# The first batch's attention probabilities turned and normalised on TensorE instead of by DMA, in a fused float32 kernel of attention and two expert layers

## The chip, the cores and the metric

The kernel runs on one core of a Trainium2 chip. The metric is the device time of one execution in microseconds (us). Engines are called by their names: TensorE (PE in the profile, its weight loads PEld), VectorE (DVE), ScalarE (ACT), GpSimd (POOL) and SyncE (SP), whose queue issues the DMAs.

## The reference

Causal attention with an additive bias from running sums, over 4 batches, 8 heads, 576 positions and 64 values a head, and then two expert layers on the 2304 tokens of 512 values, all in float32.

```python
scores = scale * np.matmul(q, k.transpose(0, 1, 3, 2))
cum = np.cumsum(np.maximum(s, 0.0), axis=-1)
bias = -(cum[:, :, :, None] - cum[:, :, None, :])
scores = np.where(causal, -1e9, scores + np.minimum(bias, 0.0))
scores = scores - np.max(scores, axis=-1, keepdims=True)
attn = np.exp(scores)
attn = attn / (np.sum(attn, axis=-1, keepdims=True) + 1e-09)
x = np.matmul(attn, v)            # then (B*S, H*D) = (2304, 512)
h = x @ w_in                      # 512 -> 2048
g = s * np.maximum(h, 0.0) ** 2 + b
x = g @ w_out                     # 2048 -> 512
return ((x @ w_a) * (x @ w_b)) @ w_out2   # 512 -> 1536 -> 512
```

## The kernel before

Nearly every product is made with operands split into a high and a low part, so that three fast matmuls stand for one float32 product. The work runs in four stages, and each stage's tail lies beside the next one's head.

*First halves.* `first_half(i)` (L596) handles the first 256 queries of group `i`; a batch has two groups of four heads, and a group two pairs of heads. So `i < 2` is the first batch, with four pairs, called pairs 0 to 3 here. For a pair, the scores of two query tiles are made (`ti = 1`: queries 128 to 255 against 256 keys; `ti = 0`: queries 0 to 127 against 128 keys), two heads each, by a float32 matmul (L626) and one that adds the mask (L627), into one PSUM bank of the tag `t_s` for each tile. VectorE takes the row maximum (L631, L635). ScalarE makes the exponentials into a float32 tile `p` (L642, tag `t_p0` with five buffers, four a pair) and their sums; VectorE makes the reciprocals `rc` (L556, L557), with a factor of 32768 in them. `split_p` (L526) multiplies the probabilities by `rc` and splits them into a high float16 part on ScalarE (L540) and a low one on VectorE (L542), both in the tile `hl` (tags `t_hl0[0]` and `t_hl0[1]`, three buffers each). SyncE then issues a DMA transpose for each query tile (L652), which puts the blocks of 128 keys by 128 queries into `tr`. The value product `av` (L576, in `value_product`, L561) multiplies `tr` by the values, split into three bfloat16 parts, and ScalarE and VectorE split its result into the expert's input `x` (L587, L589).

*Weights of the first expert.* They come as 16 slices of 1 MB; ScalarE and VectorE decode each from 64-bit numbers (L450 to L462) and split it (L470, L471). The even slices lie in the tag `t_w` before decoding, the odd ones in `t_raw`, which has one buffer.

*First expert.* For each chunk of 256 tokens and each pair of slices `h_unit` (L850, matmuls L861) makes the hidden values into a bank of `t_h`, `elementwise` (L828) squares and splits them, and `y_unit` (L868, matmuls L881) adds their product to two banks of `t_y`. Chunk 0 is the first batch's 256 queries: it needs the input `x` of all four pairs. The chunks that follow are the other batches' first queries, then the second halves (`second_half`, L708), and then the second expert follows.

The order of instructions on each engine is fixed before the kernel runs. Each piece of work is an `op` of the class `Plan` with an engine, a cost, a priority, the buffers that it reads and writes and, as `room`, further buffers that it claims. `Plan.order` plays the work through with these costs and writes the instructions out in the order in which they start there; a lower priority number goes first, and the matmuls of the first expert have 1000 added (`M`), so they yield to any attention work that is ready. A tag hands its buffers to tiles in the order of their creation, unless it says otherwise. On the chip each engine works through its own list in that order and waits by semaphores.

Of the kernel before, what the change touches and what calls it, by code (L numbers as in the profile page):

```python
# [8 lines left out]
F32 = mybir.dt.float32  # L9
# [5 lines left out]
ALU = mybir.AluOpType  # L15
# [4 lines left out]
P = 128  # L20
N = 256
# [6 lines left out]
PE, DVE, ACT, POOL, SP = "PE", "DVE", "ACT", "POOL", "SP"  # L28
# [194 lines left out]
def lin(a, b):  # L223
    return lambda n: a + b * n
# [3 lines left out]
ACT_SB, ACT_PS, ACT_EX = lin(0.30, 0.00064), lin(0.14, 0.00086), lin(0.35, 0.00086)  # L228
DVE_SB2, DVE_PS, DVE_1 = lin(0.17, 0.00102), lin(0.09, 0.00106), lin(0.10, 0.00056)
# [4 lines left out]
def fused_kernel(  # L234
# [15 lines left out]
    nc = tc.nc  # L250
# [13 lines left out]
    op = plan.op  # L264

    def as32(ap):
        return ap.bitcast(F32)
# [38 lines left out]
    t_y = tag(ps_mm, [P, 512], F32, 2, "y")  # L306
# [24 lines left out]
    ident = atc.tile([P, P], F32R, name="ident")  # L331
# [4 lines left out]
    masks, sb = Buf(None, "masks", 1), Buf(None, "sb", 1)  # L336
# [12 lines left out]
    t_hl0 = {i: tag("att0", [P, 4 * (i + 1), P], F16, 3, f"hl{i}") for i in range(2)}  # L349
# [58 lines left out]
    def light_pos(i):  # L408

        return 0.0 + 5.0 * i if i < 2 else 14.0 + 9.0 * (i - 2) if i < 4 else 50.0 + 14.0 * (i - 4)  # L410
# [185 lines left out]
    def first_half(i):  # L596

        b, g = divmod(i, 2)
        kq, rv, vt = light[i]

        def op_tiles():
            a = kq.view()
            return [a[:, j].rearrange("p (x h n) -> p x h n", x=2, h=2) for j in range(2)]

        for x in range(2):
            p = 2 * g + x
            pr = light_pos(i) + 2.5 * x
            x_t[b, p] = Buf(t_x, f"xs{b}{p}")
            tr = Buf(t_tr0, f"tr0{b}{p}")
            nm = f"0{b}{p}"  # L610

            nmx, sm, rc = (Buf(t_sm0[n], f"{n}{nm}") for n in ("nm", "sm", "rc"))
            tiles = {}
            for ti in (1, 0):
                w = (ti + 1) * P
                bank = Buf(t_s, f"s{nm}{ti}")
                at = 2 * (1 - ti)

                def view(bank=bank, w=w):
                    return bank.t.rearrange("p (h n) -> p h n", h=2)[:, :, :w]  # L620

                def go(ti=ti, w=w, x=x, view=view):
                    kt, qt = op_tiles()
                    for h in range(2):
                        o = view()[:, h]
                        nc.tensor.matmul(o, qt[:66, x, h, ti * P : (ti + 1) * P], kt[:66, x, h, :w], start=True, stop=False)  # L626
                        nc.tensor.matmul(o[:, w - P : w], ident, mask1, start=False, stop=True)  # L627

                hl = Buf(t_hl0[ti], f"hl{nm}{ti}")
                op(PE, 2 * (w / 600 + 0.08), pr, go, r=[kq, masks], w=[bank], late=0.15, room=[hl])  # L630
                op(DVE, DVE_PS(2 * w), pr, lambda at=at, nmx=nmx, view=view: nc.vector.tensor_reduce(  # L631
                    out=nmx.t[:, at : at + 2], in_=view(), axis=AX.X, op=ALU.max, negate=True
                ), r=[bank], w=[(nmx, ti)])
                tiles[ti] = w, bank, at, view, hl
            op(DVE, 0.17, pr, lambda nmx=nmx: nc.vector.tensor_scalar_mul(nmx.t, nmx.t, SCALE), w=[nmx])  # L635
            pts = {}
            for ti in (1, 0):
                w, bank, at, view, hl = tiles[ti]
                for h in range(2):
                    pt = Buf(t_p0, f"p{nm}{ti}{h}")  # L640
                    pts[ti, h] = pt
                    op(ACT, 0.25 + 0.00086 * w, pr, lambda pt=pt, h=h, at=at, view=view, nmx=nmx, sm=sm, w=w: nc.scalar.activation(  # L642
                        pt.t[:, :w], view()[:, h], AF.Exp, bias=nmx.t[:, at + h : at + h + 1], scale=SCALE,
                        accum_out=sm.t[:, at + h : at + h + 1],
                    ), r=[bank, nmx], w=[pt, (sm, at + h)], late=0.1)
            recip(rc, sm, pr)
            for ti in (1, 0):
                w, bank, at, view, hl = tiles[ti]
                for h in range(2):
                    split_p(hl, lambda hl=hl, h=h: hl.t.rearrange("p (k a h) n -> p k a h n", a=2, h=2)[:, :, :, h],  # L650
                            pts[ti, h], (rc, at + h), w, pr)
                op(SP, 1.25, pr, lambda ti=ti, tr=tr, hl=hl: nc.sync.dma_start_transpose(  # L652
                    out=tr.t.rearrange("p (k q) -> p k q", q=N)[:, : 4 * (ti + 1), (1 - ti) * P : (2 - ti) * P],
                    in_=hl.t.rearrange("p k n -> p (k n)"),
                ), r=[hl], w=[(tr, ti)], dma=49152 * 4 * (ti + 1), late=-0.9)
            value_product(b, 0, p, vt, lambda j, h, vi, x=x: vt.t[:, x, j, h, vi, :], tr, pr + 1.0)

    for i in range(2 * B):
        first_half(i)
# [162 lines left out]
    for p in range(NPAIR):  # L822
        x_t[NCK - 1, p] = Buf(t_x, f"xlast{p}")
        op(SP, 0.4, 431.0, lambda p=p: nc.sync.dma_start(as32(x_t[NCK - 1, p].t), as32(xl_dr.t[p])),
           r=[xl_dr], w=[x_t[NCK - 1, p]], dma=262144)
# [704 lines left out]
```

## Time and profile before

| | |
|---|---|
| three timed runs, median | 1007.97 us (1005.69 to 1010.25) |
| the profiled execution's own time | 1007.19 us |
| its span, first to last instruction | 1005.40 us |
| TensorE busy | 972.1 us (97%), 6664 matmuls |
| VectorE busy | 745.7 us (74%) |
| ScalarE busy | 553.4 us (55%) |
| GpSimd busy | 111.0 us (11%) |
| idle time of TensorE over the span | 33.3 us |
| mean granted clock of TensorE | 1.000 |

The span is measured from the first to the last instruction of the profiled execution; its own time is 1.79 us more. Busy time is the time in which an engine has an instruction in hand, and a busy TensorE is not TensorE at its peak. Idle time in brackets is that of the engine just before an instruction, with what ended it as the profile infers it; where the engine named had long been done, another wait ended last, often a DMA's.

### The profile page before, as it was taken

The numbers are of one execution on the slowest core, as the hardware profiler recorded it, in microseconds if no ns is written. First come the engines' busy times: TensorE is split into PE (matmuls) and PEld (weight loads), VectorE is DVE, ScalarE is ACT, GpSimd is POOL, SyncE is SP. The second block draws the span as 40 slices with busy tenths as digits, with TensorE's granted clock in tenths as the row PEclk, the third lists the DMA queues.
The fourth block names the chain that finished last, engine by engine and source line by source line (L and its number), as shares of the span: only waits on it lengthen the run. The fifth ranks groups of instructions, "written<-read, shape, count | busy, mean of one in ns | idle before, by whom it ended". The sixth has DMA issues, their size and how long they took to land.

```text
span 1005.4 us, 17274 instructions
## 1 busy us (share of the span) xinstructions
PE 972.1 (97%) x6664; PEld 872.9 (87%) x6664; DVE 745.7 (74%) x1185; ACT 553.4 (55%) x1025; POOL 111.0 (11%) x135
## 2 busy tenths in 40 slices
PE   5699999999999999999999999999999999999998
PEld 4588999999999999999988887888888788888888
DVE  6889864578879888888587627787778877777852
ACT  4679983577878778787464423333343432244431
POOL 4112001000000000000002004131223321000000
PEclk9999999999999999999999999999999999999999
DMA  8967623446676758768560113353466638997013
GB/s 231 223 162 212 185 84 69 120 111 157 146 166 153 154 134 184 150 139 152 120 214 1 63 39 110 120 213 134 170 218 212 209 136 293 377 360 256 22 64 104
DMA packets 159250, 160.13 MB, mean 159 GB/s; under 512 B 115008, under 2 KB 126016, under 8 KB 153280
## 3 DMA queue, kind: packets, MB, share of 16 engines
q1 hardware_dynamic: 159168, 159.03, 56.0%
q8 instruction: 52, 0.85, 0.4%
q14 instruction: 30, 0.25, 0.1%
HBM read 95.20 MB, written 37.52 MB: 132 GB/s over the span
## 4 chain that ended last, share of the span: by engine, by line
PE 81%; DVE 8%; ACT 4%; DMA 4%; issue 3%; POOL 1%; SPq 0%; DVEq 0%; ACTq 0%; POOLq 0%
PE h L861 15%; PE y L881 15%; PE b L1098 13%; PE pb L1320 11%; PE av L576 6%; PE yy L926 4%; PE hh L914 4%; PE s L626 3%; PE s L778 3%; PE bc L1098 2%; PE pbc L1380 2%; DMA raw_o<-in_w2o_dram 1%; DMA raw<-in_w2ab_dram 1%; DVE su L1123 1%; ACT hl L540 1%
## 5 line engine op out<-in xcount | busy, mean ns | idle before, releaser
L861 PE MATMUL h<-x_all,w 128*128 128x256 f32 x1344 | 180.3, 286 | 1.1 <-ACT r L830 1.1
L881 PE MATMUL y<-g,w 128*128 128x256 f32 x1344 | 181.0, 286 | 0.0
L861 PEld LDWEIGHTS h<-x_all,w 128*128 128x128 f32 x1344 | 168.8, 192 | 2.4 <-ACT r L830 1.3
L881 PEld LDWEIGHTS y<-g,w 128*128 128x128 f32 x1344 | 167.1, 191 | 1.5
L576 PE MATMUL av<-tr,vt 128*64 128x320 f16 (+4 forms) x1120 | 65.0, 274 | 13.1 <-ACT hl L540 6.8
L576 PEld LDWEIGHTS <-vt 128*64 128x64 bf16 x1120 | 54.7, 116 | 24.1 <-issue 9.4
L1098 PE MATMUL b<-x,wa 128*128 128x512 f32 x288 | 72.9, 390 | 0.1
L540 ACT ACTIVATE hl<-p,rc 128x256 f16<-128x256 f32 (+3 forms) x128 | 65.9, 558 | 3.8 <-DVE rc L557 3.8
L542 DVE SCALAR_TENSOR_TENSOR hl<-p,rc,hl 128x256 f16<-128x256 f32 (+3 forms) x128 | 66.2, 551 | 0.1
L1098 PEld LDWEIGHTS b<-x,wa 128*128 128x128 f32 x288 | 53.7, 188 | 11.5 <-ACT su L1133 0.5
L1098 PE MATMUL b<-x0d,ws 128*128 128x512 f32 x216 | 54.3, 392 | 1.2 <-DVE su L1123 1.2
L1098 PE MATMUL b<-x1d,ws 128*128 128x512 f32 x216 | 53.5, 390 | 0.4 <-DVE su L1123 0.4
L626 PE MATMUL s<-kq 66*128 66x256 f32 (+1 forms) x128 | 43.4, 464 | 10.2 <-POOL vt L361 7.8
L1320 PE MATMUL pb<-g,wo 128*128 128x512 f32 x216 | 50.6, 389 | 0.0
L1098 PEld LDWEIGHTS b<-x0d,ws 128*128 128x128 f32 x216 | 40.2, 188 | 11.1 <-DVE su L1123 2.3
L1098 PEld LDWEIGHTS b<-x1d,ws 128*128 128x128 f32 x216 | 40.5, 188 | 9.2 <-DVE su L1123 0.9
L783 DVE TENSOR_REDUCE nm<-s 128x1 f32<-128x512 f32 (+1 forms) x64 | 36.9, 618 | 15.6 <-PE s L779 15.6
L1320 PEld LDWEIGHTS pb<-g,wo 128*128 128x128 f32 x216 | 40.5, 188 | 8.4
L914 PE MATMUL hh<-x_all,w 128*128 128x512 f32 x192 | 46.1, 390 | 1.1 <-ACT rr L830 1.1
L830 ACT ACTIVATE r<-h 128x512 f32<-128x512 f32 x56 | 33.3, 595 | 25.0 <-PE h L861 24.7
L1133 ACT COPY su<-b 128x512 f32<-128x512 f32 x24 | 14.1, 586 | 58.5 <-PE b L1098 58.5
L926 PE MATMUL yy<-gg,w 128*128 128x512 f32 x192 | 45.6, 389 | 0.0
(382 smaller groups left out, 1926.1 us busy)
## 6 DMA issues: line engine op xcount, KB each, us to landing
raw<-in_w_dram SPq DMA_DIRECT2D x16, 1024.0 KB
raw<-in_w2ab_dram SPq DMA_DIRECT2D x12, 1024.0 KB
ab_dr<-at_all SPq DMA_DIRECT2D x24, 512.0 KB
R<-ab_dr SPq DMA_DIRECT2D x24, 512.0 KB
wo<-wo_dr SPq DMA_DIRECT2D x12, 1024.0 KB
rk<-in_k_dram SPq DMA_DIRECT2D x16, 576.0 KB
raw_o<-in_w2o_dram SPq DMA_DIRECT2D x6, 1024.0 KB
wo_dr<-wao SPq DMA_DIRECT2D x24, 256.0 KB
```

The costliest lines, as they stand in the source:

```text
L540: nc.scalar.activation(o, i_, AF.Copy, scale=r_)
L542: nc.vector.scalar_tensor_tensor(out=o, in0=i_, scalar=r_, in1=place()[:, k0:k1, 0, :cols], op0=ALU.mult, op1=ALU.subtract)
L576: nc.tensor.matmul(ap.t[64 * h : 64 * h + 64, :w], vap(j, h, vi), t[:, j, a, h, :w], start=j == 0 and m == 0, stop=j == nkt - 1 and m == 4,)
L626: nc.tensor.matmul(o, qt[:66, x, h, ti * P : (ti + 1) * P], kt[:66, x, h, :w], start=True, stop=False)
L783: op(DVE, DVE_PS(w), pr, lambda c=c, w=w, nmx=nmx, bank=banks[c]: nc.vector.tensor_reduce(out=nmx.t[:, c : c + 1], in_=bank.t[:, :w], axis ...
L830: op(ACT, 0.49, e, lambda: nc.scalar.activation(r.t.rearrange("p a n -> p (a n)"), hp.t, AF.Relu), r=[hp], w=[r], late=0.1)
L861: nc.tensor.matmul(o, w[:, wi, c, :], x_t[ck, c].t[:, xi], start=m == 0, stop=m == 3 * KC - 1)
L881: nc.tensor.matmul(o, w1_t[2 * fp + j].t[:, 1, wi, e * P : (e + 1) * P], g.t[:, gi, j], start=fp == 0 and e % 2 == 0 and j == wi == gi == ...
L914: nc.tensor.matmul(hp.t, w[:, wi, c, :], x_all[:, :, c, xi, :], start=m == 0, stop=m == 3 * KC - 1)
L926: nc.tensor.matmul(y_ps[e].t, w1_t[f].t[:, 1, wi, e * P : (e + 1) * P], g.t[:, gi].rearrange("p a n -> p (a n)"), start=f == m == 0, stop= ...
L1098: nc.tensor.matmul(o, wt.t[:, q, wi, kt * P : (kt + 1) * P], hl_of(kt, xi), start=first and n == 0, stop=last and n == 5, skip_group_check ...
L1320: nc.tensor.matmul(banks[bi][dp].t, wv(i2, wi, dp), hl.t[:, i2, xi, :], start=n_ in fresh and ip == i2 == m == 0, stop=ip == NIP - 1 and i ...
```

## The change

For the first batch (`turn = i < 2`) the probabilities aren't split before they are turned, and no DMA turns them. For each query tile and head VectorE multiplies the 128 by 128 identity by the reciprocal of each row, which gives a diagonal matrix. It lies in a tile `dg` that takes a buffer of `t_hl0[1]`. TensorE then multiplies each block of 128 queries by 128 keys of `p`, as the stationary operand, by this diagonal, in float32: the product is the block turned round and normalised, in a bank of `t_y`, one for each query tile. ScalarE copies it into the high float16 part of `tr`, and VectorE subtracts that from it for the low one. The scores claim room in `dg` instead of in `hl`. The other batches are left as they are.

```diff
+            turn = i < 2
+            dg = Buf(t_hl0[1], f"dg{nm}") if turn else None
@@ scores
-                hl = Buf(t_hl0[ti], f"hl{nm}{ti}")
-                op(PE, 2 * (w / 600 + 0.08), pr, go, r=[kq, masks], w=[bank], late=0.15, room=[hl])
+                hl = Buf(t_y if turn else t_hl0[ti], f"hl{nm}{ti}")
+                op(PE, 2 * (w / 600 + 0.08), pr, go, r=[kq, masks], w=[bank], late=0.15, room=[dg if turn else hl])
@@ after the reciprocals
-            for ti in (1, 0):
+            for ti in (1, 0) if turn else ():
+                w, bank, at, view, hl = tiles[ti]
+                dv = lambda c, dg=dg: dg.t.rearrange("p k n -> p (k n)").bitcast(F32).rearrange("p (c n) -> p c n", n=P)[:, c]
+                for h in range(2):
+                    op(DVE, 0.2, pr, lambda c=at + h, dv=dv, rc=rc: nc.vector.tensor_scalar_mul(
+                        dv(c), as32(ident), rc.t[:, c : c + 1]
+                    ), r=[rc, masks], w=[(dg, at + h)])
+
+                def go(ti=ti, at=at, hl=hl, dv=dv, pts=pts):
+                    o = hl.t.rearrange("p (k h q) -> p k h q", h=2, q=P)
+                    for h in range(2):
+                        for k_ in range(ti + 1):
+                            nc.tensor.matmul(o[:, k_, h], pts[ti, h].t[:, k_ * P : (k_ + 1) * P], dv(at + h), start=True, stop=True,
+                                             skip_group_check=True)
+
+                op(PE, 0.38 * 2 * (ti + 1), pr, go, r=[(dg, at), (dg, at + 1), pts[ti, 0], pts[ti, 1]], w=[hl], late=0.15)
+                src = lambda ti=ti, hl=hl: hl.t.rearrange("p (k h q) -> p k h q", h=2, q=P)[:, : ti + 1]
+                dst = lambda a, ti=ti, tr=tr: tr.t.rearrange("p (k a h q) -> p k a h q", a=2, h=2, q=N)[
+                    :, : ti + 1, a, :, (1 - ti) * P : (2 - ti) * P]
+                n_ = 2 * (ti + 1) * P
+                op(ACT, ACT_PS(n_), pr, lambda src=src, dst=dst: nc.scalar.copy(dst(0), src()), r=[hl], w=[(tr, (ti, 0))], late=0.1)
+                op(DVE, DVE_PS(n_), pr, lambda src=src, dst=dst: nc.vector.tensor_tensor(
+                    out=dst(1), in0=src(), in1=dst(0), op=ALU.subtract
+                ), r=[hl, (tr, (ti, 0))], w=[(tr, (ti, 1))], late=0.08)
+            for ti in () if turn else (1, 0):
```

## Rows read from the trace of the kernel before

**Rows 1.** Stretches: length, busy us (instructions) of each engine, granted clock, DMA share, GB/s.
```profile
25.00:30.00 5.00, 1.00 (x10) 1.02 (x12) 4.96 (x11) 4.92 (x10) 0.00 (x0) 1.00 1.18 171
30.00:35.00 5.00, 5.00 (x43) 4.18 (x40) 1.74 (x5) 0.77 (x2) 0.61 (x1) 1.00 0.84 207
...
70.00:80.00 10.00, 9.59 (x90) 9.17 (x88) 9.91 (x17) 9.67 (x22) 2.85 (x3) 1.00 0.78 209
...
100.00:125.00 25.00, 25.00 (x209) 24.89 (x207) 20.33 (x34) 24.45 (x52) 0.00 (x0) 1.00 0.65 192
```

**Rows 2.** TensorE in order of time: start, duration, line, tiles, count [idle before <-releaser].
```profile
7.80 1.19 PE L626 MATMUL s<-kq 66*128 66x256 f32 x2 [7.80 <-POOL vt L361]
...
19.78 1.22 PE L626 MATMUL s<-kq 66*128 66x256 f32 x2 [1.51 <-ACT p L642]
...
29.00 1.81 PE L576 MATMUL av<-tr,vt 128*64 128x256 f16 x20 [6.83 <-ACT hl L540]
...
42.55 0.80 PE L626 MATMUL s<-kq 66*128 66x128 f32 x2 [0.93 <-DVE x_all L589]
...
51.14 1.81 PE L576 MATMUL av<-tr,vt 128*64 128x256 f16 x20 [4.81 <-ACT raw L450]
...
54.36 1.81 PE L576 MATMUL av<-tr,vt 128*64 128x256 f16 x20
...
59.57 2.65 PE L861 MATMUL h<-x_all,w 128*128 128x256 f32 x11
...
64.62 1.65 PE L861 MATMUL h<-x_all,w 128*128 128x256 f32 x12
```

**Rows 3.** SyncE's queue in order of time, the DMA transposes.
```profile
19.55 9.52 SPq L652 DMA_TRANSPOSE tr<-hl  x4
...
43.41 7.77 SPq L652 DMA_TRANSPOSE tr<-hl  x4
```

**Rows 4.** In order of time: pair 0's reciprocal, and pair 1's second exponential.
```profile
16.24 0.18 DVE L557 RECIPROCAL rc<-rc 128x4 f32<-128x4 f32 x1
...
19.16 0.47 ACT L642 ACTIVATE p<-s,nm 128x256 f32<-128x256 f32 x1 [1.16 <-DVE hl L542]
```

**Rows 5.** TensorE in order of time: score and mask matmuls of single heads, early and late.
```profile
13.38 0.73 PE L626 MATMUL s<-kq 66*128 66x128 f32 x2
13.77 0.45 PE L627 MATMUL s<-mask,ident 128*128 128x128 f32 x1
14.02 0.73 PE L626 MATMUL s<-kq 66*128 66x128 f32 x2
...
74.48 0.39 PE L626 MATMUL s<-kq 66*128 66x128 f32 x2
...
74.76 0.44 PE L626 MATMUL s<-kq 66*128 66x128 f32 x2
```

**Rows 6.** In order of time: pair 1's splits, four instructions on each engine.
```profile
21.79 1.49 ACT L540 ACTIVATE hl<-p,rc 128x256 f16<-128x256 f32 x4
22.85 1.40 DVE L542 SCALAR_TENSOR_TENSOR hl<-p,rc,hl 128x256 f16<-128x256 f32 x4
```

**Rows 7.** Groups by form, 0 to 110 us: count | busy us, mean ns | idle before.
```profile
L830 ACT ACTIVATE r<-h 128x512 f32<-128x512 f32 x7 | 4.2, 593 | 0.0
...
L837 DVE TENSOR_TENSOR g<-r,g 128x512 fp32r<-128x512 f32 x6 | 4.1, 685 | 0.1
L457 DVE TENSOR_SCALAR raw<-raw 128x1024 uint32<-128x1024 uint32 x6 | 4.1, 684 | 0.0
...
L589 DVE SCALAR_TENSOR_TENSOR x_all<-av,x_all 128x256 fp32r<-128x256 f32 x8 | 3.4, 422 | 5.3 <-ACT x_all L587 5.2
L587 ACT ACTIVATE x_all<-av 128x256 fp32r<-128x256 f32 x8 | 3.1, 385 | 10.7 <-PE av L576 10.7
...
L556 DVE TENSOR_SCALAR rc<-sm 128x4 f32<-128x4 f32 x11 | 2.4, 218 | 0.0
```

**Rows 8.** TensorE's weight loads in order of time: the wait for a decoded slice.
```profile
83.35 1.26 PEld L861 LDWEIGHTS h<-x_all,w 128*128 128x128 f32 x10 [0.20 <-DVE w L471]
```

## The prediction

> **What bounds the kernel now.** I read the busy times by stretch first. From 100 us on TensorE is busy in practically every microsecond (25.00 of 25.00 in 100 to 125 us), so nothing done for the first batch can pay off there: a gain must be TensorE time won in the opening, and it reaches the end only if the later stages, which have no idle time to give back, start sooner by as much [rows 1]. The opening is different: in 25 to 30 us TensorE is busy 1.00 of 5.00 us, while VectorE (4.96) and ScalarE (4.92) are full [rows 1].
>
> Next I read TensorE's instructions in order of time. Its first score matmul starts at 7.80 us, the first product `h` of the first expert at 59.57. Between them lie four idle times: 1.51 us before 19.78, 6.83 before 29.00, 0.93 before 42.55 and 4.81 before 51.14, together 14.08 us [rows 2]. The two large ones stand before value products, of pair 0 and pair 3 of the first batch. The engines named there had long been done; what came last was the DMA transpose. SyncE's queue shows it: four transposes leave it from 19.55 to 29.07 us and four more from 43.41 to 51.18 [rows 3]. From pair 0's reciprocal (ends 16.42 [rows 4]) to its value product is 12.6 us.
>
> Third, TensorE's pace. In the opening a 128-column score pair takes 0.64 us from start to start (13.38 to 14.02), after the first `h` products 0.28 (74.48 to 74.76) [rows 5]. The granted clock is recorded as 1.00, the 2.4 GHz level, in all these stretches [rows 1], so the record doesn't show the change of pace; the starts do. From one start to the next lie three matmul instructions of 128 columns (the float32 one is issued as two, the mask as one), so one float32 matmul of 128 columns is 2/3 of that: 0.43 us at the slow pace, 0.19 at the fast one.
>
> **The change part by part.** There are four pairs (two groups of two) in the first batch.
>
> *Removed:* eight transposes and, with them, the 11.64 us (6.83 + 4.81) of idle time before pair 0's and pair 3's value products. SyncE's queue loses eight issues; the loads for the second batch stand behind less. I count these loads at nothing further: the scores that need them are in the same TensorE queue behind the work costed here. Also removed are, for each pair, the four splits on ScalarE (1.49 us in a run) and the four on VectorE (1.40 us) [rows 6].
>
> *Added on TensorE:* six float32 matmuls of 128 columns for each pair (two heads by one plus two key blocks), 24 in all. Slow pace: 24 x 0.43 = 10.2 us; fast pace: 24 x 0.19 = 4.6. The diagonal product is a float32 matmul like the score's, so I take the score's row; everything up to the first `h` ran at the slow pace, so I take 10.2. Before the change this path held no TensorE work, and there is no cover for it beyond the idle time that it replaces.
>
> *Added on VectorE:* four products of the identity with a column, 128 by 128. The nearest rows are 0.22 us for 4 columns (fixed cost) and 0.68 for 1024, which gives an estimate of 0.24 each [rows 7]. Then two subtractions out of PSUM, 512 and 256 columns: 0.69 and 0.42 by the nearest rows. Together 4 x 0.24 + 1.11 = 2.07 us against 1.40 removed: +0.7 a pair, +2.7 in all. *On ScalarE:* two copies out of PSUM, 0.59 and 0.39 [rows 7], 0.98 against 1.49: -0.5 a pair, -2.0 in all. VectorE is full in 25 to 30 us but has 3.3 us free in the five after [rows 1]; those are waits for TensorE's scores, so I take the 2.7 as hidden. Were it not, it would delay the first expert's weights by up to that much.
>
> *Moved:* the probabilities (five buffers, four for each pair) are now let go by TensorE instead of by VectorE. Already before, pair 1's exponential waited 1.16 us for pair 0's split [rows 4]; it will now wait for pair 0's turning, which stands in TensorE's queue behind other pairs' scores. The turned tile takes both banks of `t_y`, so the next pair's turning waits until VectorE's subtraction has run, in a queue with the weights' decoding between. The trace shows no such wait; its nearest rows are TensorE's waits of 1.51 us for an exponential and 0.93 for a subtraction [rows 2]. Four hand-overs cost between 0 and about 4 x 3.5 us (as much as the idle time now). They can't cost below nothing, as each is a wait. I take two waits of the larger size, 3.0 us, since TensorE mostly has another pair's scores to do meanwhile.
>
> *Order:* the order on each engine is written out by a planner from costs that take TensorE at its fast pace. With the first batch done sooner, some of the second batch's work that stood before the first `h` (from 54.36 to 59.57 a value product and pair 3's scores, and before that half a pair's scores at two heads by 0.64: some 6.5 us [rows 2, 5]) may come behind it and run at the fast pace, saving 0 to 3.2 us. I take 2.0.
>
> The sum from 7.80 us on: idle 14.1 goes, 10.2 of turning and 3.0 of new waits come, 2.0 saved by the pace: 10.2 + 3.0 - 14.1 - 2.0 = -2.9 us. The profiled execution took 1007.19 us (span 1005.40 and 1.79 around it), 0.8 below the median of the three timed runs, 1007.97. 1007.19 - 2.9 = 1004.3; the forecast is **1004.5 us**, in a range of its own of 1001.5 to 1007.
>
> By a rule of the Trainium skill the transposes would not be worth removing: "DMA: Bandwidth & Descriptors", section Latency and other measured facts, gives a DMA transpose an effective 261 GB/s, by which pair 0's 0.39 MB would be an estimated 1.5 us. The trace disagrees, with 9.4 us from the first issue to the value product [rows 2, 3]; by the page nearly all of the 10.2 would be a loss.
>
> **The rivals.**
>
> *The fast pace comes early.* If dense turning, or an earlier first `h`, brings TensorE to its fast pace some 10 us sooner, half of ten microseconds of scores and value products is won as well, 5 us on top: 1007.2 - 2.9 - 5 = about 999.5. For it: the pace changed between the first `h` matmuls (11 in 2.65 us from 59.57) and the next ones (12 in 1.65 from 64.62), so it may be `h` that brings it, and `h` may come sooner [rows 2]. Against it: from 7.80 to 18.27 us TensorE had no idle time, with the same kind of float32 matmul, and stayed slow [rows 2, 5]. The Trainium skill ("TensorE: Matmul & The Clock Gate", Part 1) says that sustained activity releases the throttle; by that the opening scores would have done it already, and the trace does not agree. Chance 0.32.
>
> *The weights' decoding takes the gain.* An `h` product waited 0.20 us for a slice's last subtraction at 83.35 us [rows 8], and VectorE is busy 9.91 of 10 us in 70 to 80 [rows 1]. If VectorE's extra 2.7 us stand in its full stretches, the slices come no sooner and TensorE waits at 80 us for what it won at 55: 1007 us, 1005.5 to 1008.5. Against it: VectorE's idle time in 30 to 35 us, which was waiting for TensorE. Chance 0.16.
>
> *Slower: each turning waits in turn.* Exponentials wait for the previous pair's turning, that for VectorE's diagonal, that for the reciprocal: if TensorE has nothing else at its queue's head, four waits of about 3.5 us leave the idle time where it was, and the 10.2 us come on top, less the 2.0 of moved work: 1007.2 + 10.2 - 2.0 = about 1015. It decides from the point where the new waits exceed 14.1 + 2.0 + 5 - 10.2 = 10.9 us, 2.7 a pair. For it: both banks and four of five buffers are held by one pair. Against it: TensorE had a later pair's scores at hand until 18.27 us (19.78 less 1.51), two microseconds past pair 0's reciprocal [rows 2, 4]. Chance 0.12.
>
> *It doesn't do what it says* (the wait was not the transposes' but SyncE's queue's, which stays): pair 0's value product would wait nearly as long. That it would leave more than half the wait is hard to see with no transposes before it; it is within the slower case.
>
> **How the numbers follow.** Half a percent is 5.0 us, about what a measurement of this kernel can tell from no change. Forecast 0.40 (all within it), early fast pace 0.32 (faster), decoding 0.16 (within), slower 0.12. So faster 0.32, same 0.56, slower 0.12. The range of 998 to 1010.5 us takes the forecast, the decoding case, most of the early-pace case, and the forecast with 9 us of new waits at its upper end; it leaves out the slower case and the best quarter of the early one.
>
> **What would show it.** Right: value products of pairs 0 and 3 with less than 2 us idle before them; 24 pairs of new matmul instructions at 0.43 us, so some 10 us more TensorE work before the first `h`; that `h` at 52 to 58 us instead of 59.57; TensorE's idle time over the span down by about 10 us. Wrong: the new matmuls at 0.19 us or scores at 0.28 us a head before the first `h` (early pace); idle times before the turning of over 2.7 us each (slower); new idle time in 60 to 100 us before `h` with a weight slice as releaser (decoding).

## The result and the profile after

The changed kernel takes 1018.34 us (median; 1012.42 to 1020.33) beside 1007.81 (1005.69 to 1010.25) of the kernel before in the same series: 1.0101 of it, with an interval of 1.0081 to 1.0121. It is slower by one per cent, where the forecast was 1004.5 us, in a range of 998 to 1010.5. The profiled execution took 1020.33 us with a span of 1018.5; TensorE is busy for 978.4 us of it (972.1 before) and idle for 40.1 (33.3 before), where its idle time was to fall by about 10.

In the changed kernel scores are L628, the diagonals L653, the turning matmuls L661, value products still L576; from there on lines have moved by 26 (`h` is L887). First TensorE in order of time (start, duration, line, tiles, count, idle before it and its releaser); it answers [rows 2, 5].

```profile
18.14 2.79 PE L661 MATMUL hl<-dg,p 128*128 128x128 f32 x12
20.77 0.60 PE L628 MATMUL s<-kq 66*128 66x256 f32 x2
...
23.58 1.58 PE L661 MATMUL hl<-dg,p 128*128 128x128 f32 x12 [0.88 <-DVE dg L653]
25.76 1.01 PE L576 MATMUL av<-tr,vt 128*64 128x256 f16 x20 [0.61 <-ACT p L644]
...
29.68 1.60 PE L661 MATMUL hl<-dg,p 128*128 128x128 f32 x12
31.12 0.47 PE L628 MATMUL s<-kq 66*128 66x128 f32 x2
...
36.30 1.58 PE L661 MATMUL hl<-dg,p 128*128 128x128 f32 x12 [2.33 <-DVE dg L653]
...
44.43 1.67 PE L576 MATMUL av<-tr,vt 128*64 128x256 f16 x20 [1.83 <-ACT p L644]
46.03 2.58 PE L887 MATMUL h<-x_all,w 128*128 128x256 f32 x12
```

In the opening the long waits of value products for transposes are gone (0.61 us for pair 0, 1.83 for pair 3), the fast pace comes right after the first turning (2.63 us from its start to the next instruction, 1.44 for the third), and the first `h` starts at 46.03 instead of 59.57. Part of that is work of the second batch that now stands behind it, but the rest was won, and was lost again further on. The stretches show the first place (columns as in [rows 1]):

```profile
25.00:30.00 5.00, 3.71 (x50) 3.22 (x49) 4.93 (x13) 4.10 (x14) 0.12 (x1) 1.00 0.73 171
30.00:35.00 5.00, 3.97 (x30) 3.57 (x28) 5.00 (x8) 2.20 (x9) 2.82 (x3) 1.00 0.01 2
60.00:70.00 10.00, 9.57 (x44) 9.00 (x44) 8.85 (x18) 7.63 (x19) 1.80 (x4) 0.57 0.11 22
70.00:80.00 10.00, 7.29 (x66) 6.62 (x67) 4.89 (x11) 5.20 (x12) 1.56 (x3) 0.83 1.00 309
100.00:125.00 25.00, 23.39 (x178) 22.88 (x177) 20.77 (x34) 22.30 (x48) 0.00 (x0) 0.93 0.53 176
```

TensorE is idle for 2.71 us from 70 to 80 (0.41 before) and for 1.61 from 100 to 125 (none before), and its granted clock, 1.00 in these stretches before, is 0.57 from 60 to 70 us: a mean that lies between the two levels, 1.2 GHz (0.50) and 2.4. The view also gives 1.00 where the trace holds no clock record at all: the first record is at 62.75 us in the kernel before and at 20.73 in the changed one. So the 1.00 of the opening [rows 1] tells nothing of the clock there; the starts of the instructions show the slow pace.

Among what TensorE waits for from 60 to 160 us are the first expert's weights, 2.2 us of 7.7 in all (2.0 in all before, none of it for weights; waiting line, what it waited for: us in sum, times, longest):

```profile
PE h L887 <- DVE w L471: 1.4, 2, 0.8
...
PE h L887 <- ACT w L470: 0.8, 1, 0.8
```

The first of the next two fences shows, in order of time, the kernel before; the second the changed one. The rows are the copy of the row sums (L510) and, for the first expert's slices, ScalarE's last cast (L470) and VectorE's last subtraction (L471).

```profile
26.19 0.42 DVE L510 CAST sums_hl<-sums 32x576 fp32r<-32x576 f32 x1
...
39.46 1.13 ACT L470 CAST w<-raw 128x1024 fp32r<-128x1024 f32 x1
40.81 1.22 DVE L471 TENSOR_TENSOR w<-raw,w 128x1024 fp32r<-128x1024 f32 x1
```

```profile
30.39 1.22 DVE L471 TENSOR_TENSOR w<-raw,w 128x1024 fp32r<-128x1024 f32 x1
46.05 0.42 DVE L510 CAST sums_hl<-sums 32x576 fp32r<-32x576 f32 x1
46.41 1.16 ACT L470 CAST w<-raw 128x1024 fp32r<-128x1024 f32 x1
47.61 1.23 DVE L471 TENSOR_TENSOR w<-raw,w 128x1024 fp32r<-128x1024 f32 x1
```

The second slice is ready 6.8 us later than before, and the last of the sixteen too (160.21 instead of 153.45). The copy L510 stands just ahead of its cast. The code says why they go together: weight buffers (`t_w`) are given out in the order in which they are named, `sums_hl` is named just before the second slice, so the planner places nothing that writes that slice before the copy has its place; and the copy has a late due number (the planner's priority), 30. By the planner's own costs, played through for both kernels, VectorE runs out of other ready work once in the order of before (idle for 0.17 us), and there the copy starts, at 22.7 us. In the changed order it has work with lower numbers without a gap from 13 us on, so the copy comes at 42.1, and the second slice's cast on ScalarE, whose data are decoded at 30.0, is placed at 42.1 with it.

The second place is far behind, at the start of the last stage's products `pb`, here of the kernel before and then of the changed one:

```profile
870.14 8.35 PE L1320 MATMUL pb<-g,wo 128*128 128x512 f32 x36
```

```profile
877.16 5.86 PE L1346 MATMUL pb<-g,wo 128*128 128x512 f32 x25
887.16 4.38 PE L1346 MATMUL pb<-g,wo 128*128 128x512 f32 x11 [4.15 <-DVE g L1295]
```

From there on both kernels have the same order of instructions on every engine. So every run below is also read in two parts: where the first `pb` starts, and how long it is from there to the end of the span.

| run | median us | ratio to before, 95% | L510 | 2nd slice | first `h` | first `pb` | from `pb` to end |
|---|---|---|---|---|---|---|---|
| before | 1007.81 | | 26.2 | 40.8 | 59.6 | 870.1 | 135.3 |
| after | 1018.34 | 1.0101 [1.0081, 1.0121] | 46.1 | 47.6 | 46.0 | 877.2 | 141.3 |
| e1 turning, old order | 1007.59 | 1.0007 [0.9985, 1.0029] | 29.8 | 40.7 | 58.1 | 866.7 | 138.2 |
| e2 DMA, new order | 1022.98 | 1.0146 [1.0113, 1.0178] | 54.3 | 55.6 | 53.0 | 886.2 | 135.3 |
| e3 no turning, old order | 1004.25 | 0.9972 [0.9954, 0.9990] | 26.3 | 38.7 | 56.3 | 868.6 | 135.3 |
| e4 before, other order | 1012.22 | 1.0052 [1.0033, 1.0071] | 26.6 | 44.7 | 49.4 | 873.5 | 142.1 |
| e5 after, L510 earlier | 1010.57 | 1.0026 [1.0004, 1.0047] | 32.4 | 41.5 | 44.6 | 872.3 | 135.3 |
| e6 after, slice ahead | 1012.92 | 1.0049 [1.0031, 1.0068] | 56.5 | 38.8 | 47.0 | 871.0 | 140.3 |
| e7 after, less decoding | 1015.18 | 1.0070 [1.0035, 1.0104] | 44.3 | 46.6 | 45.0 | 872.6 | 140.3 |
| e8 after again | 1018.01 | 1.0101 [1.0073, 1.0128] | 46.6 | 47.9 | 45.5 | 876.1 | 140.3 |
| e9 before, less decoding | 1006.87 | 0.9996 [0.9973, 1.0020] | 25.8 | 37.6 | 57.2 | 867.2 | 135.3 |
| e10 = e3 and e9 | 1002.81 | 0.9942 [0.9920, 0.9963] | 25.7 | 38.0 | 55.8 | 864.6 | 135.3 |
| e11 e1, GpSimd | 1012.84 | 1.0048 [1.0026, 1.0070] | 29.9 | 45.9 | 65.1 | 874.2 | 140.0 |
| e12 e1, turned twice | 1011.13 | 1.0041 [1.0020, 1.0063] | 33.1 | 44.9 | 61.8 | 877.3 | 135.3 |
| e13 before, L510 late | 1013.16 | 1.0067 [1.0043, 1.0090] | 46.6 | 50.3 | 49.4 | 876.1 | 135.3 |
| e14 before again | 1008.08, one run | | 26.2 | 40.2 | 59.6 | 871.0 | 135.3 |

The last five columns (us) are from the one profiled execution of each: starts of L510 and of the second slice's last subtraction on VectorE, starts of the first `h` and `pb` on TensorE, and the span less that `pb`. The kernel before had medians of 1006.98, 1006.82, 1007.13 and 1006.06 us in the series of e1 to e4, e5 to e8, e9 to e12, and e13 and e14. A profiled execution need not lie at the median: that of e4 took 1017.35 us, the longest of its ten.

### The profile page after: what moved, and what is told of

Same layout as the page of the kernel before. It is cut to its first block, busy times and chain, and to the rows that moved or that the text cites. A ratio compares the mean times of both kernels' runs of the same rounds, so it can differ in the third digit from the quotient of the medians.

```text
span 1018.5 us, 17367 instructions
## 1 busy us (share of the span) xinstructions
PE 978.4 (96%) x6712; PEld 879.6 (86%) x6712; DVE 746.9 (73%) x1193; ACT 544.9 (54%) x1017; POOL 111.6 (11%) x135
## 4 chain that ended last, share of the span: by engine, by line
PE 37%; DVE 6%; DMA 6%; issue 3%; ACT 2%; SPq 0%; POOL 0%; DVEq 0%; ACTq 0%
PE b L1124 12%; PE pb L1346 11%; PE yy L952 4%; PE hh L940 3%; PE bc L1124 2%; DMA raw_o<-in_w2o_dram 2%; PE pbc L1406 2%; DMA ab_dr<-at_all 2%; PE y L907 1%; PE h L887 1%; DMA raw<-in_w2ab_dram 1%; DVE wa L1051 1%; DVE su L1149 1%; DMA R<-ab_dr 1%; DVE x1d L1058 1%
## 5 line engine op out<-in xcount | busy, mean ns | idle before, releaser
L907 PE MATMUL y<-g,w 128*128 128x256 f32 x1344 | 184.7, 289 | 1.4 <-DVE g L863 1.4
L887 PE MATMUL h<-x_all,w 128*128 128x256 f32 x1344 | 178.5, 286 | 3.3 <-DVE w L471 1.4
L887 PEld LDWEIGHTS h<-x_all,w 128*128 128x128 f32 x1344 | 168.9, 194 | 4.9 <-DVE w L471 1.8
L907 PEld LDWEIGHTS y<-g,w 128*128 128x128 f32 x1344 | 170.4, 194 | 3.1 <-DVE g L863 1.6
L576 PE MATMUL av<-tr,vt 128*64 128x320 f16 (+4 forms) x1120 | 62.5, 267 | 8.6 <-DMA tr<-hl 4.6
L576 PEld LDWEIGHTS <-vt 128*64 128x64 bf16 x1120 | 54.3, 112 | 17.2 <-issue 5.7
L540 ACT ACTIVATE hl<-p,rc 128x512 f16<-128x512 f32 (+3 forms) x112 | 58.7, 574 | 6.2 <-DVE rc L557 4.2
L542 DVE SCALAR_TENSOR_TENSOR hl<-p,rc,hl 128x512 f16<-128x512 f32 (+3 forms) x112 | 59.2, 569 | 3.5 <-ACT hl L540 3.0
L856 ACT ACTIVATE r<-h 128x512 f32<-128x512 f32 x56 | 33.5, 598 | 38.7 <-PE h L887 33.5
L1346 PEld LDWEIGHTS pb<-g,wo 128*128 128x128 f32 x216 | 41.5, 193 | 13.3 <-DVE g L1295 4.6
L1124 PEld LDWEIGHTS b<-x0d,ws 128*128 128x128 f32 x216 | 40.2, 188 | 11.1 <-DVE su L1149 2.4
L952 PE MATMUL yy<-gg,w 128*128 128x512 f32 x192 | 46.1, 390 | 1.0 <-DVE gg L872 1.0
L628 PE MATMUL s<-kq 66*128 66x256 f32 (+1 forms) x128 | 37.0, 410 | 10.4 <-DMA kq<-sums 7.9
L459 DVE SCALAR_TENSOR_TENSOR raw<-raw 128x1024 uint32<-128x1024 uint32 x28 | 34.3, 1224 | 16.6 <-ACT raw L453 12.9
L940 PE MATMUL hh<-x_all,w 128*128 128x512 f32 x192 | 45.9, 390 | 0.2 <-DMA x_all<-xl_dr 0.2
```

Source lines behind the costliest of these rows:

```text
L459: op(DVE, 1.15, pr, lambda: nc.vector.scalar_tensor_tensor(out=lo(), in0=hi(), scalar=0x80000000, in1=lo(), op0=ALU.bitwise_and, op1=ALU.b ...
L540: nc.scalar.activation(o, i_, AF.Copy, scale=r_)
L542: nc.vector.scalar_tensor_tensor(out=o, in0=i_, scalar=r_, in1=place()[:, k0:k1, 0, :cols], op0=ALU.mult, op1=ALU.subtract)
L576: nc.tensor.matmul(ap.t[64 * h : 64 * h + 64, :w], vap(j, h, vi), t[:, j, a, h, :w], start=j == 0 and m == 0, stop=j == nkt - 1 and m == 4,)
L887: nc.tensor.matmul(o, w[:, wi, c, :], x_t[ck, c].t[:, xi], start=m == 0, stop=m == 3 * KC - 1)
L907: nc.tensor.matmul(o, w1_t[2 * fp + j].t[:, 1, wi, e * P : (e + 1) * P], g.t[:, gi, j], start=fp == 0 and e % 2 == 0 and j == wi == gi == ...
```

## The experiments

### The turning and the order, apart (e1 to e4)

e1 has the changed kernel's instructions in the order of the kernel before: the planner sees the old operations, and the new instructions are issued at their places.

```
-  split_p(hl, ...)                      # ScalarE, VectorE
+  turned(ti, h, hl, tr, pts, rc, w, pr) # at the high split's place: matmuls, copy; at the low's: subtraction
-  lambda: nc.sync.dma_start_transpose(...)
+  lambda: None if turn else nc.sync.dma_start_transpose(...)
```

> The turning instructions of the change, but every instruction in the order that the planner wrote for the kernel before: the diagonals stand right behind the reciprocals, the turning matmuls and the copy where the high split stood, the subtraction where the low split stood, and the transposes' places stay empty. Theory A (the loss is in the new order of the instructions that the planner writes when it sees the turning): 1000 to 1009 us, about before's 1008 or better. Theory B (the loss is in the turning itself: its TensorE work and the pace that it lifts and lets fall): 1013 to 1020 us, as the changed kernel.

e2 is the opposite: splits and DMA transposes of before, at the places of the changed kernel's order (with two more buffers for probabilities, and one tile more).

```
-  nc.tensor.matmul(o[:, k_, h], pts[ti, h]..., dv(at + h), ...)
+  # nothing; at the copy's place the high splits, at the subtraction's:
+  split(1); nc.sync.dma_start_transpose(out=tr..., in_=tile_of()...)
```

> The other way about: splits and DMA transposes as before, but every instruction in the order that the planner wrote for the changed kernel; the probabilities get seven buffers instead of five and the split tiles of the lower queries a tag of their own, since the new order frees them at other places. Theory A (the new order is the loss): 1012 to 1022 us. Theory B (the turning itself is): 1005 to 1010 us, about before's 1008.

e3 keeps the order of before and leaves out the transposes: the split probabilities are written straight into `tr`.

```
+  split_p(..., straight(ti, h, tr), ...)
+  lambda: None if free else nc.sync.dma_start_transpose(...)
```

> Before's order, the first batch's splits written straight into the tile that the value product reads, and neither transposes nor turning matmuls: the blocks of the first batch reach the value product unturned. It bounds what doing away with the transposes can bring. If TensorE's idle time before the value products of pairs 0 and 3 is what bounds the opening, as the prediction held: 11.6 us or nearly so, 996 to 999 us. If the weights' decoding bounds it: 1003 to 1008 us.

e4 changes nothing but one planned cost of the kernel before, by which another order comes out.

```
-  op(SP, 1.25, pr, lambda ...: nc.sync.dma_start_transpose(
+  op(SP, 1.0 if i < 2 else 1.25, pr, lambda ...: nc.sync.dma_start_transpose(
```

> The kernel before with one number of the planner's changed: the cost that it books on SyncE's queue for the first batch's transposes is 1.0 us instead of 1.25, so it may write another order with the same instructions. Theory A (order alone moves this kernel by about a percent): it may lie anywhere from 1003 to 1020 us, more than 3 us from before if the order differs in the opening. Theory B: within 3 us of before, 1005 to 1011 us.

The turning in the old order costs nothing measurable (1007.59 beside 1006.98), and the old transposes in the new order lose even more than the changed kernel (1022.98). So the loss is in the order, not in the turning. The clock doesn't part them either: by the clock records TensorE is at the lower level, after its first rise and before the first `pb`, for 20.5 us in e1 and for 20.5 and 17.1 in the two profiles of the changed kernel (after, e8). e4 confirms the weight of the order from outside: another order, made by a quarter of a microsecond in one planned cost, is worth 5.2 us (its second slice is 3.9 us later too, though its copy L510 stays early).

e3 corrects the largest term of the prediction. With no transposes of the first batch, and nothing in their place, only 2.7 us of 1007 go (1006.98 to 1004.25), where 11.6 or nearly so was expected if the idle time bounded the opening. TensorE's idle times in e3, before the first `h`:

```profile
19.90 1.22 PE L626 MATMUL s<-kq 66*128 66x256 f32 x2 [1.51 <-ACT p L642]
24.96 0.80 PE L626 MATMUL s<-kq 66*128 66x128 f32 x2 [0.93 <-ACT p L642]
31.89 1.19 PE L626 MATMUL s<-kq 66*128 66x256 f32 x2 [3.65 <-DMA raw<-in_w_dram]
40.35 0.79 PE L626 MATMUL s<-kq 66*128 66x128 f32 x2 [0.94 <-DVE x_all L589]
46.17 0.79 PE L626 MATMUL s<-kq 66*128 66x128 f32 x2 [0.29 <-ACT p L642]
50.03 1.81 PE L576 MATMUL av<-tr,vt 128*64 128x256 f16 x20 [2.32 <-ACT hl L540]
52.87 1.22 PE L626 MATMUL s<-kq 66*128 66x256 f32 x2 [1.03 <-DVE x_all L589]
```

They add up to 10.67 us, after 14.08 before [rows 2]: other waits have taken the place of those for transposes. Most of the named ones are for work of VectorE and ScalarE; for the longest, 3.65 us, the profile names a weight load, which the scores don't read, so what ended it is open. The stretches of e3 and, in the second fence, of e10 (below) show these two engines:

```profile
20.00:30.00 10.00, 7.32 (x52) 5.76 (x52) 9.83 (x20) 10.00 (x26) 1.15 (x1) 1.00 1.06 262
```

```profile
20.00:30.00 10.00, 7.11 (x52) 5.55 (x51) 8.89 (x19) 10.00 (x24) 1.11 (x1) 1.00 0.95 167
```

### The place of one copy (e5, e6, e13)

Two ways to part the second slice from the late copy, in the changed kernel: e5 gives the copy an earlier due number, e6 names the slice's buffer first.

```
-  op(DVE, 0.4, 30.0, lambda: nc.vector.tensor_copy(hl()[:, 0], sum_row(1)), ...   # L510
+  op(DVE, 0.4, 21.0, lambda: nc.vector.tensor_copy(hl()[:, 0], sum_row(1)), ...   # e5
```

```
-        if f == 1:
-            sums_hl = Buf(t_w, "sums_hl")
         w1_t[f] = Buf(t_w, f"w1_{f}")
         split_w(raws[f], w1_t[f], ...)
+        if f == 1:
+            sums_hl = Buf(t_w, "sums_hl")                                            # e6
```

> The changed kernel with one number other: the planner's due number of the row sums' first copy (the cast into sums_hl, L510) is 21 and not 30. The weight buffers are given out in the order in which they are named, and sums_hl is named before the first expert's second slice w1; so no instruction that writes w1 can be placed before this copy. In the changed kernel the copy ran at 46.05 us (26.19 before) and w1's own copy on ScalarE right behind it, at 46.41 (39.46 before). Theory A (the loss is in the order: this copy's late place holds back the weights of the first expert): the copy runs at about 30 to 35 us, w1's last subtraction at 38 to 42 instead of 47.6, the end of the first expert comes 5 to 7 us sooner (517 to about 511), and the time is 1006 to 1012 us. Rival (the early fast pace of TensorE is given back when its granted clock falls after 40 us, whatever the weights do): the weights come sooner but the time stays at 1015 to 1020.

> The changed kernel with the buffer of sums_hl named behind that of w1 instead of ahead of it, all due numbers as they are: the row sums' copy may be as late as it likes, and w1 need not wait for its place. Theory A (the loss is w1's place behind that copy): as with the earlier copy, w1's last subtraction at 36 to 42 us, time 1006 to 1012 us. If only the copy itself mattered (the second batch's row sums, which its scores need), nothing is gained: 1015 to 1020. Rival (clock): 1015 to 1020 too.

e13 does the reverse in the kernel before, with its transposes: the copy is made late.

```
-           behind=last_rows[5:6])
+           behind=last_rows[6:7])
```

> The kernel before, transposes and all, with one number other: the row sums' first copy (into sums_hl, L510) is put behind the seventh of the loads of its rows on SyncE's queue and not the sixth, by which the planner places it some 35 places later on VectorE. The mirror of the earlier cast in the changed kernel. Theory A (the late place of this one copy, which holds back w1's place and with it all slices, is most of the loss of the changed kernel): the copy runs at 46 to 55 us instead of 26.19, w1's last subtraction at 48 to 58 instead of 40.81, the end of the first expert 5 to 10 us later, the time 1012 to 1018 us. Rival (the loss hangs on what the turning does, and the earlier cast only happened to give another good order): 1005 to 1009.

The second slice and the copy in e6:

```profile
38.77 1.22 DVE L471 TENSOR_TENSOR w<-raw,w 128x1024 fp32r<-128x1024 f32 x1
56.49 0.44 DVE L510 CAST sums_hl<-sums 32x576 fp32r<-32x576 f32 x1
```

e5 and e13 came out in the theory's range, e6 0.9 us above it. e5 gives back 7.4 us of the 11.2 (1018.01 to 1010.57 in one series), e6 5.1. In e6 the copy is later than ever, at 56.5 us, and the second slice early, at 38.8: it is the slice's place that counts, not the copy's. And e13 loses 7.1 us by one number on a copy of 0.44 us, without any turning:

```profile
46.59 0.44 DVE L510 CAST sums_hl<-sums 32x576 fp32r<-32x576 f32 x1
46.94 1.11 ACT L470 CAST w<-raw 128x1024 fp32r<-128x1024 f32 x1
...
50.27 1.22 DVE L471 TENSOR_TENSOR w<-raw,w 128x1024 fp32r<-128x1024 f32 x1
```

Each of these edits lets the planner write the rest anew as well. Compared by the traces, 1028 of VectorE's 1104 instructions ahead of the first `pb` keep their order in e6, but only 661 in e5, and 660 of 1097 in e13 (619 between before and after). So e6 is the clean one of the three; in e5 and e13 other places in the order may have a share.

The sizes at the end of the first expert, however, were not all those expected. Its last matmul starts at 517.2 and 517.7 us in the two profiles of the changed kernel, at 515.1 in e5 (about 511 was expected) and at 511.3 in e6; at 510.7 and 511.7 in those of before, and at 515.6 in e13, 3.9 to 4.9 later (5 to 10 expected). By the start of the first `pb`, e5 is 4.8 us ahead of the changed kernel's first profile and 3.8 ahead of its second, e6 6.2 and 5.1, and e13 is 6.0 and 5.1 behind the two profiles of the kernel before. So e6 is back at the place of the kernel before there. It has the late wait still; e5 has not, and takes 135.3 us instead of 140.3 or 141.3 from `pb` to the end. The falling clock is no rival for e6's gain: before its first `pb` TensorE is at the lower level for 30.7 us, longer than in the changed kernel.

### The amount of decoding (e7, e9, e10)

e7 and e9 leave out the last of VectorE's decoding instructions for each of the first expert's slices, in the changed kernel and in that of before; e10 does so in e3.

```
-  op(DVE, 1.15, pr, lambda: nc.vector.scalar_tensor_tensor(out=hi(), in0=hi(), scalar=3, in1=lo(), ...
+  op(DVE, 1.15, pr, lambda: None if any(raw is r_ for r_ in raws.values()) else nc.vector.scalar_tensor_tensor(...
```

> The changed kernel with its own order of instructions, and one of VectorE's three decoding instructions left out for each of the first expert's 16 slices (the third, L459/L462: shift and or), some 1.1 us each, so the weights' values are not the reference's. Theory A (TensorE waits from 60 to 160 us for slices that VectorE decodes too late): VectorE has 16 to 18 us less to do there, the last slice's subtraction comes from 160 to about 152 or sooner, the end of the first expert from 517 to about 510 or sooner, and the time is 1006 to 1012 us. Rival (clock, or TensorE's own work): less than 3 us are won, 1015 to 1018.

> The kernel before, its order of instructions kept, with one of VectorE's three decoding instructions left out for each of the first expert's 16 slices (L459/L462, some 1.1 us each), so the weights' values are not the reference's. Theory D (what TensorE wins in the opening is taken by slices that come when their decoding is done, in the kernel before as well): VectorE has some 18 us less to do up to 155 us, the end of the first expert comes 2 to 4 us sooner than 510.7, and the time is 1003 to 1005 us. Rival (TensorE alone bounds the kernel from 60 us on, as its full windows say): less than 1 us, 1006 to 1008.

> The kernel before without the transposes of the first batch (the probabilities' parts reach the value product as they are, not turned round, nothing takes the transposes' place) and without one of VectorE's three decoding instructions for each of the first expert's slices; order of instructions kept, neither result is the reference's. Alone, the first of the two gave 1004.25 us (2.8 less than before). Theory D (the opening's gain is held back by the slices): with both holds gone, more is won than by the two one by one: 998 to 1001 us. Rival (the opening's idle time was worth only 2.8 us for another reason, TensorE's own clock among them): the two add up at most, 1002 to 1005.

Some 17 us less for VectorE (107.9 us busy up to 165 us in e7, 124.8 in the changed kernel) win 2.8 us in the changed kernel, not clear of noise with e7's five times, and nothing measurable in that of before; the theory had 6 to 12 and 2 to 4. So the amount of VectorE's work is not most of what makes the slices late; the place in the queue counts for more: a shorter chain that stands behind the same others comes nearly as late (second slice at 46.6 instead of 47.9). e10 wins 4.3 us by the medians, and 5.8 by its ratio (3.7 to 8.1). e3's 2.7 and e9's 0.3 give that within their intervals, so nothing calls for the theory that the slices hold back what e3 wins; e10 doesn't exclude it. In e10 the wait at 31.6 us is as long as in e3 (3.58 us) with VectorE no longer full, 8.89 of 10 us, and ScalarE still so, 10.00 of 10: on this evidence ScalarE's queue is what comes next behind the transposes, though no run took work off ScalarE.

### The price of the turning itself (e11, e12)

Both start from e1. e11 makes the diagonals on GpSimd, e12 issues each turning matmul twice.

```
-  nc.vector.tensor_scalar_mul(dv[:, h], as32(ident), rc.t[:, c : c + 1])
+  nc.gpsimd.tensor_scalar_mul(dv[:, h], as32(ident), rc.t[:, c : c + 1])     # e11
-            for z in range(2):
+            for z in (0, 1, 0, 1):                                            # e12
```

> The turning in the order of the kernel before (1007.59 us in the first series), with the 16 products of the identity with a column on GpSimd and not on VectorE. If VectorE's time up to 60 us is on the path (the diagonals are 16 x 0.24 = 3.8 us of it, in front of the weights' decoding): 1004 to 1006.5 us. If the hand-over from VectorE's reciprocal to GpSimd and its slower pace delay the turning, and that is on the path: 1008 to 1011. If neither is: 1007 to 1008.

> The turning in the order of the kernel before, with each of the 24 float32 matmuls issued twice (the second writes the same values again): the price of the TensorE work that the change adds, by itself. The prediction's step (it lies on the path, with no cover but the idle time that it replaces): 24 x 0.19 to 24 x 0.43 = 4.6 to 10.2 us more than the 1007.59 of the single turning, 1012 to 1018. Theory D (TensorE waits for the slices up to 80 us and beyond, and what it does before is covered by that): 0 to 2 us more, 1007 to 1010.

Twenty-four matmuls more cost 3.5 us (1007.59 to 1011.13, in two series). That lies between the 4.6 to 10.2 of the prediction's step and the 0 to 2 of the other theory; with the two intervals of the table it is an estimated 0.3 to 6.5, so it excludes neither, only the upper part of the first. The two profiles lie further apart, 10.6 us at the first `pb`. On GpSimd four diagonals take 2.35 to 4.45 us, on VectorE mostly 0.87, and TensorE waits for them:

```profile
16.20 2.35 POOL L683 TENSOR_SCALAR hl<-ident,rc 128x128 f32<-128x128 f32 x4 [3.52 <-DVE rc L557]
...
30.05 4.45 POOL L683 TENSOR_SCALAR hl<-ident,rc 128x128 f32<-128x128 f32 x4 [4.11 <-DVE rc L557]
```

The time goes up by 5.2 us, to 1.8 above the 1008 to 1011 expected if the hand-over and GpSimd's slower pace lie on the path. So what taking the diagonals off VectorE gives, by the expectation 3.8 us of its work, is less than what the longer chain from reciprocal to value product brings with it. How much of the 5.2 is the chain itself is open. The granted clock in e11 is 0.50 from 30 to 50 us (0.86 and 0.84 in e1's two stretches there), and its profile has the late wait.

### The late wait (e8, e14)

Both kernels once more, word for word, with nothing edited.

> The changed kernel once more, word for word. What is asked is whether TensorE's late wait of 4.15 us for VectorE's g at 887 us, which the first profile of it shows and that of before does not, is there in every execution. If it belongs to the kernel: 4 us again at the same place, and the time 1018. If it is chance of one execution: no such wait or a smaller one in this profile, and the span is 4 us shorter than 1018.5.

> The kernel before once more, word for word, for one look: whether TensorE's late wait of 3 to 4 us for VectorE's g, near 880 us, which both profiles of the changed kernel show, is absent again. If it hangs on the order of the opening: absent, span 1003 to 1007 us. If it is chance of an execution: it can be there here too.

The late wait is in both profiles of the changed kernel and in neither of before:

```profile
885.05 4.33 PE L1346 MATMUL pb<-g,wo 128*128 128x512 f32 x11 [3.10 <-DVE g L1295]
```

It is also in e1, e4, e6, e7 and e11, and not in e2, e3, e5, e9, e10, e12 and e13: e4 has no turning and has it, e5 and e12 turn and don't. SyncE's queue shows where it begins. First the kernel before, then the changed one:

```profile
844.73 1.78 SPq L1200 DMA_DIRECT2D wo_dr<-wso  x4
...
855.86 8.31 SPq L1262 DMA_DIRECT2D R<-ab_dr  x6
```

```profile
851.75 2.30 SPq L1226 DMA_DIRECT2D wo_dr<-wso  x4
...
863.55 12.56 SPq L1288 DMA_DIRECT2D R<-ab_dr  x6
```

The stores of `wso` leave at the same distance from the first `pb` (25.4 us), yet from there things take longer: the six loads behind them leave within 12.56 us instead of 8.31, as they wait 7.0 us and not 4.4 for a store to land. Why a store lands later in some profiles stays open. It was seen that this belongs to neither the turning nor the order of that stage. It may differ from execution to execution too: e11's ten times fall into two groups, 1009.33 to 1011.47 and 1014.21 to 1016.37, and its profiled one, with the wait, is of the upper group. That is not shown, as one trace is kept of each run.

## Why the prediction was wrong

*The order.* This is the step that failed in sign. The prediction knew that a planner writes the order and took 2.0 us of gain from work that moves behind the first `h`. The order alone made 10.4 us of loss (e8 less e1, 1018.01 to 1007.59). About half of it hangs on one place: the second slice behind a copy that became late because VectorE, in the planner's account, no longer had a gap for it. e6 gives back 5.1 us with little else moved; e5 gives back 7.4 and e13 loses 7.1 in the kernel before, both with more of the order rewritten. In the profiles 5.1 to 7.0 us of the changed kernel's loss are there at the first `pb`, and 5.0 to 6.0 come behind it, with the late wait, whose cause is open.

*The idle time removed.* The sum takes off all 14.1 us. The prediction's own list of what is removed has only the 11.64 before the value products of pairs 0 and 3; the other 2.44, waits for an exponential and a subtraction, went in without a reason. The 11.64 were counted as gone because the transposes ended last. They were not the only thing that TensorE waited for: without any transposes 10.67 us remain and the time falls by 2.7. The evidence was in the prediction's own first part, VectorE and ScalarE full from 25 to 30 us [rows 1]; it was used as a bound for what the change adds, not as the next wait. "Where a stall goes, what is late next" was not asked of the main term.

*The turning.* 10.2 us on TensorE without cover became about 7.2 in the trace (2.63, 1.58, 1.44 and 1.58 for the four pairs), as the fast pace came at the end of the first pair's; added a second time they cost 3.5, with the wide interval above. At the fast pace a float32 matmul took 0.24 us (12 instructions in 1.44), not the 0.19 read from the scores. With the removed time at 2.7 instead of 14.1 the two nearly cancel: e1, which has both, is 0.6 us above the kernel before.

*The small terms* held in the main. Four diagonals take 0.87 us in two of the four pairs and 1.17 and 2.48 in the others (0.96 foreseen). The waits in front of the turnings, 0.88 and 2.33, are 3.2 us in sum (3.0 foreseen), but that is luck: the profile names the diagonals in VectorE's queue, and the 3.0 stood for probabilities and banks that come free late. Value products of pairs 0 and 3 wait less than 2 us, as foreseen.

*The rivals.* The early fast pace came true as a mechanism: from the second pair on turnings take 1.6 us, and three of the four value products 1.0 instead of 1.8 [rows 2]. It brought no gain: TensorE ran out of work, and the granted clock fell (0.57 from 60 to 70 us). What the fall costs by itself was not tried; e1, where the clock is at the lower level for as long, is no slower than the kernel before. The Trainium skill ("TensorE: Matmul & The Clock Gate", Part 1) has sustained activity release the throttle; the traces agree only in part. In the kernel before 10 us of scores without a gap, from 7.80 us on, did not do it, and in e2 not even 12.6, from 7.50 on; in the changed kernel the clock rose at 20.73, at the end of the first turning. Whether the kind of the work did it or that it went on longer, no run tells. The rival of the weights' decoding saw rightly that TensorE would wait for slices; it looked for the cause in VectorE's extra 2.7 us, and by e7, where 17 us less win 2.8, the amount matters little. The slower rival forecast a time, 1015 us, that is near the one measured, by luck, as its mechanism isn't there: no turning of the changed kernel waits more than 2.33 us.

## What to carry to other kernels

Where a planner writes the order, lay the new order beside the old one before any term is priced, and look for the instructions that moved far: here the place of one weight slice behind a copy of 0.4 us, moved by 20 us, weighed more than 24 matmuls or eight transposes. Buffers that are given out in the order in which they are named tie together work that has nothing to do with each other, so the first question to a late instruction is which buffer it stands in line for. And a wait that ends with a transfer is worth only the distance to the next thing that would have held the same instruction; full engines beside the idle one were the sign here that this distance is short.

## What was not expected of the hardware

TensorE's pace did not change in 12.6 us of unbroken float32 scores with 66 rows (e2, 7.50 to 20.1 us). In every profile with a turning the clock's first record, a rise to 1.00, is at 19.67 to 22.49 us, during the first turning with 128 rows or, in e5, e7 and e8, in the work just behind it; in those without it is at 52 to 65, behind the start of the first `h`. In every profile with a turning, and in some with another order only (e2, e4, e13), the clock then falls again in places (0.50 from 50 to 60 us in e1). The four diagonals of the first pair took VectorE 2.48 us, in the changed kernel and in e1, those of most other pairs 0.87. GpSimd needs 0.6 to 1.1 us for a 128 by 128 product that VectorE mostly does in 0.22.
